# Attention, soft MoE and a gated layer on one core: one conversion step on GpSimd for two units, expert weights in 12 KB pieces, and a new place for the last rows' transposes

## The chip, the cores and the metric

One core of a Trainium2 chip runs the whole program. The metric is the device time of one execution in microseconds; the kernel before takes 594.82 us (median of 3 runs, 594.3 to 595.8). The core has five engines with instruction queues of their own, each run in order: PE (TensorE, matrix products and transposes, results in PSUM), DVE (VectorE), ACT (ScalarE), POOL (GpSimd, which here works on SBUF alone) and SP (SyncE, which here issues all the transfers).

## The reference

Three layers, one behind the other:

```python
# 1. causal attention: q, k, v are (4, 12, 448, 64)
attn = softmax(mask(q @ k.T / 8)) @ v            # -> x, (1792, 768)
# 2. soft MoE: phi (768, 32), w1 (8, 768, 1024), w2 (8, 1024, 768)
logits = x @ phi
slots  = softmax(logits, axis=0).T @ x           # 32 slots, 4 for each expert
so     = relu(slots[e] @ w1[e]) @ w2[e]          # for each of 8 experts
x      = softmax(logits, axis=1) @ so
# 3. gated layer: w_gate, w_val (768, 1536), w_out (1536, 768), given as float64
out    = (sigmoid(x @ w_gate) * (x @ w_val)) @ w_out
```

The factors that setup_inputs draws with make the weights of the third layer doubles; the kernel gets them as pairs of 32-bit words.

## The kernel before

**Attention (0 to 256 us).** Two heads make a pair, and 24 pairs run one behind the other, six for each batch. Every step of a pair (transposes of q and k `Tq`, `Tk`; their scaling to 16 bits `hq`, `hk` on ACT and the residuals `lq`, `lk` on DVE; scores; mask and row minimum `m` on DVE; exponential `e` on ACT; transposes of the probabilities `P0` to `P3` on PE with copies `C0` to `C3` out of PSUM; product with v `V`, `VZ`; two more transposes `Xa`, `Xb`) has a time in the table `AT` (L82 to L85), counted from the start of its pair. Pairs are 9.0 units apart (`II`, L81). All steps of all pairs are sorted by these times (L627) and issued in that order with every instruction pinned, so the table is the program order of each engine; only the order counts, not the values. The scores of a pair come in two lots: `S1Z` (256 keys, and the last 64 rows against 448) and `S20` (384 and 128 keys). `P3` is the transposes of the last rows. The copies C0 to C3 go to ACT or DVE by `PTE` (L79): C3 is ACT's in even pairs and DVE's in odd ones. P0 to P3, the logits `L` and the first transposes of a tail share two PSUM buffers in turn. `L` (L462) adds up the router's logits for three pairs, `LT` (L469) copies (ACT, first half of a batch) or adds them (DVE, second half). After six pairs a batch's `tail` (L506) makes the slot softmax and the sums over tokens in thirteen steps whose times stand in `TAIL` (L89).

**Expert weights (258 to 346 us).** `load_w` (L173) loads w1 and w2 in 32 transfers of 1.5 MB, each half an expert's matrix, into a ring of buffers; ten are issued during attention, the others as buffers come free. In a transfer a partition gets 3 rows of w1 (4 KB each, 128 rows apart) or 4 rows of w2 (3 KB each). For each expert, four products at a time stand side by side in PE's columns (L757 to L777). Unit 0's weights of the third layer are loaded ahead of expert 6.

**Third layer (347 to 595 us).** The 1536 hidden columns are cut into six units of 256. A unit's three matrices (`o`, `v`, `g`, 1.5 MB of doubles each, as 128 x 1536 doubles) are converted by `from_f64` (L186) in four steps: ACT builds the low word from 16 bits, ACT multiplies the high word (L196), then two bit operations on DVE (L198, L200), all in place, on every second 32-bit word. Then stage t multiplies: `gate` (L834) makes the hidden values with their 16-bit halves `hhi`, `hlo` (POOL subtracts, L852), and `outp` (L854) multiplies for each of 14 token tiles and adds into `oacc`. By `EV` (L93) the eviction is ACT's in stage 0; later it is DVE's, or ACT's with an addition on POOL (L880). While stage t runs, unit t+1 is converted. Here the order on each engine is not pinned: a planner with its own costs fixes it when the program is built.

Of the kernel before, what the change touches and what calls it, by code (L numbers as in the profile page):

```python
# [7 lines left out]
F32 = mybir.dt.float32  # L8
# [6 lines left out]
ALU = mybir.AluOpType  # L15
# [5 lines left out]
def kernel(  # L21
# [13 lines left out]
    nc = tc.nc  # L35
# [6 lines left out]
    KC = DM // 128  # L42
# [18 lines left out]
    for g, (b, h0, n) in enumerate(GRP):  # L61
        for o in range(0, n, 2):
# [18 lines left out]
    II = 9.0  # L81
    AT = dict(Tq=0.0, Tk=0.02, hk=2.66, hq=3.87, lq=4.08, lk=4.52, S1Z=6.23, m10=6.29, m11=6.34, e10=7.23, e11=7.59, mZ=7.62,  # L82
              S20=9.01, m21=10.53, m01=11.87, m00=12.14, m20=12.45, e21=13.29, e01=13.43, e00=13.47, e20=13.54, P1=13.62,
              P0=14.04, eZ=14.34, C1=15.02, C0=15.43, r=15.45, P2=15.48, P3=16.0, ri=16.52, C3=17.53, C2=18.31, V=20.55,
              VZ=20.86, xu=23.04, Xa=23.34, xn=24.26, Xb=26.29, xT=26.32, L=27.71, LT=29.3)  # L85
    LOADS = dict(q=-25.5, k=-25.4, w=-6.0, v=-1.0)
    SCALES = (-16.0, -15.0, -14.0, -11.0, -10.0, -9.0, -4.0, -2.9)
    copy = {"A": nc.scalar.copy, "V": nc.vector.tensor_copy, "P": nc.gpsimd.tensor_copy}
    TAIL = (30.3, 31.6, 32.3, 33.4, 34.6, 35.7, 41.2, 42.4, 43.6, 44.7, 46.5, 49.0, 51.0)  # L89
    PINW = True  # L90
    PB = (3, 3, 2)
    HIE = 'VAVAAAVAAAVV'
    EV = 'AAPVVPVVVPVV'  # L93
    MWE = 'AAAAAA'
    WHE = 'VVAAAV'


    const = ctx.enter_context(tc.tile_pool(name="const", bufs=1))
# [4 lines left out]
    ident = const.tile([128, 128], F32, name="ident")  # L103
# [10 lines left out]
    g = nc.gpsimd  # L114
# [27 lines left out]
    def mult(on, out, in_, x):  # L142
        if on == "A":
            nc.scalar.activation(out=out, in_=in_, func=AF.Copy, scale=x)  # L144
        else:
            nc.vector.tensor_scalar(out, in_, x, None, ALU.mult)
# [9 lines left out]
    worder = []  # L156
    for e in range(E):
        if e == E0:
            for u in PARTS[0]:
                worder += w_unit(u)  # L160
        for r in range(2):
            worder.append((("1", e, r), w1[e].rearrange("(k p) f -> p k f", p=128)[:, 3 * r:3 * r + 3, :], 3))
        for r in range(2):
            worder.append((("2", e, r), w2[e].rearrange("(k p) f -> p k f", p=128)[:, 4 * r:4 * r + 4, :], 4))
    n_ab = len(worder)
    for u in range(len(PARTS[0]), FF // UC):
        worder += w_unit(u)
# [1 line left out]
    wt = {}  # L169
# [16 lines left out]
    def from_f64(key):  # L186

        t = wt[key].bitcast(I32).rearrange("p a (b w) -> p a b w", w=2)  # L190
        lo, hi = t[:, :, :, 0], t[:, :, :, 1]
        top = wt[key].bitcast(U16).rearrange("p a (b w) -> p a b w", w=4)[:, :, :, 1]

        nc.scalar.activation(out=lo, in_=top, func=AF.Copy, scale=2.0 ** -13, bias=2.0 ** -15 - 0.5)  # L194
        yield
        mult("A", hi.bitcast(F32), hi.bitcast(F32), 2.0 ** -112)  # L196
        yield
        nc.vector.scalar_tensor_tensor(lo, hi, -2 ** 31, lo, ALU.bitwise_and, ALU.bitwise_or)  # L198
        yield
        nc.vector.scalar_tensor_tensor(hi, hi, 3, lo, ALU.logical_shift_left, ALU.bitwise_or)  # L200
        yield
        return hi.bitcast(F32)


    with ExitStack() as actx:
# [17 lines left out]
        acc = ac_p.tile([128, DM], F32, name="acc")  # L223
# [28 lines left out]
        fin = {}  # L252
# [8 lines left out]
        xu = x_p.tile([128, 512], F32, name="xu")  # L261
# [330 lines left out]
        for i in range(NP):  # L592
# [13 lines left out]
            for c in range(4):  # L606
                at(t0 + AT[f"P{c}"], st_P, i, c)
                at(t0 + AT[f"C{c}"], st_C, i, c)
            for x, f in (("r", st_r), ("ri", st_ri), ("V", st_V), ("VZ", st_VZ), ("xu", st_xu), ("Xa", st_Xa), ("xn", st_xn),
                         ("Xb", st_Xb), ("xT", st_xT)):  # L610
# [4 lines left out]
            if i % NPB == NPB - 1:  # L615
                gen([t0 + x for x in TAIL], tail, i // NPB)
        for g in range(NG):
# [12 lines left out]
        slotT = const.tile([128, KC, NS], F32, name="slotT")  # L630
        p4 = psT.tile([128, KC, NS], F32, tag="t", name="psm4")
        for kc in range(KC):
            nc.tensor.matmul(p4[:, kc], lhsT=acc[:, 128 * kc:128 * kc + 128], rhs=fin["fw"], start=True, stop=True)
        nc.vector.tensor_copy(slotT, p4)


# [120 lines left out]
    for e in range(E):  # L757
        ps = ps1.tile([128, 256], F32, tag="a", name="psh")
        for kc in range(KC):
            w = wt["1", e, kc // 3]  # L760
            for g in range(4):
                nc.tensor.matmul(ps[32 * g:32 * g + 32, :], lhsT=slotT[:, kc, :],  # L762
                                 rhs=w[:, kc % 3, 256 * g:256 * g + 256], start=kc == 0, stop=kc == KC - 1)
        hm = hm_p.tile([128, 256], F32, tag="hm", name="hm")
        nc.vector.tensor_scalar(hm, ps, 0.0, emask[:, e:e + 1], ALU.max, ALU.mult)
        pt = ps1.tile([128, 2, 128], F32, tag="b", name="psht")
        for i in range(2):
            nc.tensor.transpose(pt[:, i], hm[:, 128 * i:128 * i + 128], ident)  # L768
        hT = hm_p.tile([128, 2, 128], F32, tag="hT", name="hT")
        nc.scalar.copy(hT, pt)  # L770
        for f in range(8):
            g, i = divmod(f, 2)
            w = wt["2", e, f // 4]
            for c in range(3):
                nc.tensor.matmul(so[32 * c:32 * c + 32, :], lhsT=hT[:, i, 32 * g:32 * g + 32],  # L775
                                 rhs=w[:, f % 4, 256 * c:256 * c + 256],
                                 start=e == 0 and f == 0, stop=e == E - 1 and f == 7)  # L777
        if e < B:
            b = e
            cs = cs_p.tile([128, 4, 2, 2, NS], F32, tag="cs", name="cs")  # L780
            chi = hm_p.tile([128, 4, NS], F32R, tag="chi", name="chi")
            c = call[:, b]
            nc.vector.tensor_copy(chi, c)
            ch = chi.bitcast(F32).rearrange("p j (o s) -> p j o s", o=1).to_broadcast([128, 4, 2, NS])
            c4 = c.rearrange("p j (o s) -> p j o s", o=1).to_broadcast([128, 4, 2, NS])
            nc.vector.tensor_copy(cs[:, :, :, 0, :], ch)
            nc.vector.tensor_tensor(cs[:, :, :, 1, :], c4, ch, ALU.subtract)
            ps = ps1.tile([128, S], F32, tag="b", name="psc")
            for j, (s0, n) in enumerate(CH):
                nc.tensor.transpose(ps[:, s0:s0 + n], cs[:n, j].rearrange("p a b s -> p (a b s)"), ident[:n, :n])  # L790
            nc.scalar.copy(cT[:, b * S:(b + 1) * S], ps)
        if e == E0 - 1:
            once.close()
            wo0 = ctx.enter_context(rp("wo0", 1))
            wo_p.update({u: wo0 for u in PARTS[0]})
            w0 = {}
            for u in PARTS[0]:
                for nm in "ovg":
                    f = from_f64((nm, u))
                    while True:  # L800
                        try:
                            next(f)
                        except StopIteration as x:
                            w0[nm, u] = x.value
                            break
                for _ in prep_o(u, w0["o", u]):
                    pass
    sos = hm_p.tile([96, 256], F32, tag="sos", name="sos")
    nc.vector.tensor_copy(sos, so)
    pt = ps1.tile([128, 2, 96], F32, tag="b", name="psst")  # L810
# [148 lines left out]
```

## Time and profile before

| | |
|---|---|
| median of 3 runs | 594.82 us |
| the profiled execution | 596.93 us, its span 595.0 us |
| PE busy | 514.5 us (86%) |
| DVE busy | 390.0 us (66%) |
| ACT busy | 322.6 us (54%) |
| POOL busy | 238.7 us (40%) |
| chain that ended last | PE 63%, ACT 15%, DMA 7%, DVE 5%, issue 3%, POOL 2% |
| moved by DMA | 101.59 MB in 95566 packets, 171 GB/s over the span |

Shares are averages over three stages of different kinds, so a row is read with its stage. The chain of waits is followed back from the last instruction to whatever released each step. Line L244 stands for every pinned instruction of attention, so these are told apart by the names of their tiles: `psS` are scores, `psP` transposes of probabilities, `PT` their copies, `nm` row minima, `psL` and `LT` logits.

### The profile page before, as it was taken

The numbers are of one execution on the slowest core, as the hardware profiler recorded it, in microseconds if no ns is written. First come the engines' busy times: TensorE is split into PE (matmuls) and PEld (weight loads), VectorE is DVE, ScalarE is ACT, GpSimd is POOL, SyncE is SP. The second block draws the span as 40 slices with busy tenths as digits, with TensorE's granted clock in tenths as the row PEclk, the third lists the DMA queues.
The fourth block names the chain that finished last, engine by engine and source line by source line (L and its number), as shares of the span: only waits on it lengthen the run. The fifth ranks groups of instructions, "written<-read, shape, count | busy, mean of one in ns | idle before, by whom it ended". The sixth has DMA issues, their size and how long they took to land.

```text
span 595.0 us, 12947 instructions
## 1 busy us (share of the span) xinstructions
PE 514.5 (86%) x4971; PEld 317.2 (53%) x4971; DVE 390.0 (66%) x943; ACT 322.6 (54%) x738; POOL 238.7 (40%) x333
## 2 busy tenths in 40 slices
PE   2899989998999899799935689679999989899997
PEld 1576756665667566465512235344554445455654
DVE  3688877886878687331027038986895958675664
ACT  2577767776777577301043049996865843334300
POOL 6654663656365410000000014206696760355720
PEclk9899999999999899979995789998999979799999
DMA  7746557464774313779999993713505303000044
GB/s 161 200 106 170 167 160 199 129 144 133 199 196 115 91 33 107 287 251 391 405 397 405 405 400 137 281 38 119 200 1 209 110 2 107 0 1 1 2 185 186
DMA packets 95566, 101.59 MB, mean 171 GB/s; under 512 B 68625, under 2 KB 68625, under 8 KB 95505
## 3 DMA queue, kind: packets, MB, share of 16 engines
q1 hardware_dynamic: 95504, 100.77, 51.3%
q8 instruction: 39, 0.64, 0.5%
q14 instruction: 23, 0.18, 0.1%
HBM read 95.26 MB, written 5.51 MB: 169 GB/s over the span
## 4 chain that ended last, share of the span: by engine, by line
PE 63%; ACT 15%; DMA 7%; DVE 5%; issue 3%; POOL 2%; SPq 1%; ACTq 0%; DVEq 0%; POOLq 0%
PE pso L870 22%; PE psP L244 9%; PE psS L244 8%; DMA w<-in_moe_w_dram 6%; ACT P L244 4%; PE psX L244 4%; PE psT L244 4%; PE psh L762 3%; PE so L775 3%; ACT hi L244 3%; ACT oacc L144 2%; ACT w L194 2%; PE psg L688 2%; PE psg L843 1%; ACT w L144 1%
## 5 line engine op out<-in xcount | busy, mean ns | idle before, releaser
L852 POOL TENSOR_TENSOR hlo<-hs,hhi 128x448 f16<-128x448 f32 x48 | 59.2, 1241 | 174.9 <-DVE hhi L851 132.5
L870 PE MATMUL pso<-wh,hhi 128*128 128x384 f16 (+1 forms) x384 | 111.5, 338 | 8.1 <-ACT oacc L144 7.6
L870 PE MATMUL pso<-wl,hhi 128*128 128x384 f16 (+1 forms) x384 | 110.3, 334 | 0.0
L870 PE MATMUL pso<-wh,hlo 128*128 128x384 f16 (+1 forms) x384 | 107.8, 331 | 2.6 <-POOL hlo L852 2.6
L244 ACT ACTIVATE P<-psS,nm 128x256 f32<-128x256 f32 (+3 forms) x168 | 82.0, 504 | 31.4 <-PE psP L244 16.6
L870 PEld LDWEIGHTS <-hhi 128*128 128x128 f16 (+1 forms) x768 | 63.5, 103 | 63.8 <-issue 32.3
L244 DVE CUSTOM_DVE_ANT_0 psS<-psS,cmaskq,sc 128x256 f32<-128x256 f32 (+1 forms) x144 | 66.5, 489 | 32.7 <-PE psS L244 30.2
L882 DVE SCALAR_TENSOR_TENSOR oacc<-pso,osc,oacc 128x384 f32<-128x384 f32 x98 | 58.7, 613 | 35.1 <-PE pso L870 34.6
L244 PE MATMUL psP<-ident,P 128*128 128x128 f32 x384 | 59.6, 288 | 17.7 <-ACT P L244 11.6
L880 POOL TENSOR_TENSOR oacc<-oacc,ev 128x384 f32<-128x384 f32 x42 | 55.0, 1321 | 23.1 <-ACT ev L144 23.0
L244 PEld LDWEIGHTS psP<-ident,P 128*128 128x128 f32 x384 | 41.3, 142 | 35.9 <-ACT P L244 21.5
L244 POOL TENSOR_TENSOR sq<-sq 128x512 bf16<-128x512 bf16 (+1 forms) x88 | 56.3, 640 | 6.5
L244 PE MATMUL psV<-PT,v 128*64 128x64 f32 (+3 forms) x672 | 48.0, 293 | 0.3 <-ACT PT L244 0.3
L870 PEld LDWEIGHTS <-hlo 128*128 128x128 f16 (+1 forms) x384 | 34.1, 102 | 26.1 <-issue 3.5
L198 DVE SCALAR_TENSOR_TENSOR w<-w 128x1536 int32<-128x1536 int32 x18 | 33.7, 1874 | 14.5 <-ACT w L144 14.1
L244 PEld LDWEIGHTS psV<-PT,v 128*64 128x64 f32 x672 | 32.0, 137 | 20.9 <-issue 14.0
L144 ACT ACTIVATE ev<-pso,osc 128x384 f32<-128x384 f32 x42 | 23.6, 581 | 27.4 <-PE pso L870 23.7
L194 ACT ACTIVATE w<-w 128x1536 int32<-128x1536 uint16 x18 | 30.2, 1680 | 14.9 <-DMA w<-in_moe_w_out_dram 7.9
L244 POOL TENSOR_SCALAR r<-sum 128x7 f32<-128x7 f32 x24 | 5.9, 244 | 79.1 <-ACT P L244 71.9
L762 PE MATMUL psh<-w,slotT 128*32 128x256 f32 x384 | 29.9, 441 | 7.8 <-DMA w<-in_moe_w_dram 7.3
L244 ACT ACTIVATE hi<-psT,qks 128x448 f16<-128x448 f32 x48 | 27.8, 630 | 15.2 <-PE psT L244 15.2
L770 ACT COPY hT<-psht 128x256 f32<-128x256 f32 x8 | 3.0, 372 | 61.0 <-PE psht L768 61.0
(233 smaller groups left out, 1000.7 us busy)
## 6 DMA issues: line engine op xcount, KB each, us to landing
w<-in_moe_w_dram SPq DMA_DIRECT2D x32, 1536.0 KB, 9.3
w<-in_moe_w_out_dram SPq DMA_DIRECT2D x6, 1536.0 KB, 12.2
w<-in_moe_w_val_dram SPq DMA_DIRECT2D x6, 1536.0 KB, 13.4
w<-in_moe_w_gate_dram SPq DMA_DIRECT2D x6, 1536.0 KB, 6.7
out_dram<-oacc SPq DMA_DIRECT2D x14, 384.0 KB, 2.3
q<-in_q_dram SPq DMA_DIRECT2D x36, 128.0 KB, 3.0
k<-in_k_dram SPq DMA_DIRECT2D x36, 128.0 KB, 2.9
v<-in_v_dram SPq DMA_DIRECT2D x36, 128.0 KB, 8.0
```

Of the source, the lines that this page charges most:

```text
L144: nc.scalar.activation(out=out, in_=in_, func=AF.Copy, scale=x)
L194: nc.scalar.activation(out=lo, in_=top, func=AF.Copy, scale=2.0 ** -13, bias=2.0 ** -15 - 0.5)
L198: nc.vector.scalar_tensor_tensor(lo, hi, -2 ** 31, lo, ALU.bitwise_and, ALU.bitwise_or)
L244: x = f(*a, **kw)
L688: nc.tensor.matmul(ps[32 * g:32 * g + 32, :], lhsT=soT[:, kc], rhs=w[:, kc], start=kc < 4, stop=kc + 4 >= KC)
L762: nc.tensor.matmul(ps[32 * g:32 * g + 32, :], lhsT=slotT[:, kc, :], rhs=w[:, kc % 3, 256 * g:256 * g + 256], start=kc == 0, stop=kc == KC - 1)
L775: nc.tensor.matmul(so[32 * c:32 * c + 32, :], lhsT=hT[:, i, 32 * g:32 * g + 32], rhs=w[:, f % 4, 256 * c:256 * c + 256], start=e == 0 and ...
L843: nc.tensor.matmul(pg, lhsT=d["g"][:, cols], rhs=cT[:, b * S:(b + 1) * S], start=True, stop=True)
L852: nc.gpsimd.tensor_tensor(lo[:, c], hs, hi[:, c], ALU.subtract)
L870: nc.tensor.matmul(ps[n][o:o + m], lhsT=hid[b, u][x][:, c, s0:s0 + m], rhs=y[:, c, 384 * n:384 * n + 384], start=f, stop=l)
L880: nc.gpsimd.tensor_tensor(a, a, x, ALU.add)
L882: nc.vector.scalar_tensor_tensor(a, ps[n], osc, a, ALU.mult, ALU.add)
```

## The change

It has three parts, and changes nothing in what is computed.

1. `AT`: P3 moves from 16.0 to 18.015, behind S20 of the next pair (18.01) and ahead of Tk of the pair after it (18.02); C3 moves from 17.53 to 18.6, behind C2; LT moves from 29.3 to 30.6, from ahead of hk and the masks of 128 to between hk and hq and behind the four mask steps. The first five `TAIL` times move back by 0.2 to 1.0: the transpose `psl` from ahead of Xa to behind S1Z, the exponential `eT` from ahead of C0 to behind it.
2. Expert weights: a partition gets 3 (w1) or 4 (w2) neighbouring rows, 12 KB in one piece. Which row lies in which partition changes, so the slots' columns (stride 3), the columns of w1 that form a group (pairs, stride 4) and the columns that are transposed (stride 2) change with it.
3. `from_f64`: for units 1 and 2 the second step is POOL's, not ACT's (six instructions on 128 x 1536 words).

```diff
--- before.py
+++ after.py
@@ -81,18 +81,19 @@
     II = 9.0
     AT = dict(Tq=0.0, Tk=0.02, hk=2.66, hq=3.87, lq=4.08, lk=4.52, S1Z=6.23, m10=6.29, m11=6.34, e10=7.23, e11=7.59, mZ=7.62,
               S20=9.01, m21=10.53, m01=11.87, m00=12.14, m20=12.45, e21=13.29, e01=13.43, e00=13.47, e20=13.54, P1=13.62,
-              P0=14.04, eZ=14.34, C1=15.02, C0=15.43, r=15.45, P2=15.48, P3=16.0, ri=16.52, C3=17.53, C2=18.31, V=20.55,
-              VZ=20.86, xu=23.04, Xa=23.34, xn=24.26, Xb=26.29, xT=26.32, L=27.71, LT=29.3)
+              P0=14.04, eZ=14.34, C1=15.02, C0=15.43, r=15.45, P2=15.48, P3=18.015, ri=16.52, C3=18.6, C2=18.31, V=20.55,
+              VZ=20.86, xu=23.04, Xa=23.34, xn=24.26, Xb=26.29, xT=26.32, L=27.71, LT=30.6)
     LOADS = dict(q=-25.5, k=-25.4, w=-6.0, v=-1.0)
     SCALES = (-16.0, -15.0, -14.0, -11.0, -10.0, -9.0, -4.0, -2.9)
     copy = {"A": nc.scalar.copy, "V": nc.vector.tensor_copy, "P": nc.gpsimd.tensor_copy}
-    TAIL = (30.3, 31.6, 32.3, 33.4, 34.6, 35.7, 41.2, 42.4, 43.6, 44.7, 46.5, 49.0, 51.0)
+    TAIL = (31.3, 31.95, 33.3, 33.9, 34.8, 35.7, 41.2, 42.4, 43.6, 44.7, 46.5, 49.0, 51.0)
     PINW = True
     PB = (3, 3, 2)
     HIE = 'VAVAAAVAAAVV'
     EV = 'AAPVVPVVVPVV'
     MWE = 'AAAAAA'
     WHE = 'VVAAAV'
+    ONP = (1, 2)
 
 
     const = ctx.enter_context(tc.tile_pool(name="const", bufs=1))
@@ -159,9 +160,9 @@
             for u in PARTS[0]:
                 worder += w_unit(u)
         for r in range(2):
-            worder.append((("1", e, r), w1[e].rearrange("(k p) f -> p k f", p=128)[:, 3 * r:3 * r + 3, :], 3))
+            worder.append((("1", e, r), w1[e].rearrange("(r p k) f -> r p k f", r=2, k=3)[r], 3))
         for r in range(2):
-            worder.append((("2", e, r), w2[e].rearrange("(k p) f -> p k f", p=128)[:, 4 * r:4 * r + 4, :], 4))
+            worder.append((("2", e, r), w2[e].rearrange("(r p k) f -> r p k f", r=2, k=4)[r], 4))
     n_ab = len(worder)
     for u in range(len(PARTS[0]), FF // UC):
         worder += w_unit(u)
@@ -193,7 +194,10 @@
 
         nc.scalar.activation(out=lo, in_=top, func=AF.Copy, scale=2.0 ** -13, bias=2.0 ** -15 - 0.5)
         yield
-        mult("A", hi.bitcast(F32), hi.bitcast(F32), 2.0 ** -112)
+        if key[1] in ONP:
+            nc.gpsimd.tensor_scalar(hi.bitcast(F32), hi.bitcast(F32), 2.0 ** -112, None, ALU.mult)
+        else:
+            mult("A", hi.bitcast(F32), hi.bitcast(F32), 2.0 ** -112)
         yield
         nc.vector.scalar_tensor_tensor(lo, hi, -2 ** 31, lo, ALU.bitwise_and, ALU.bitwise_or)
         yield
@@ -630,7 +634,9 @@
         slotT = const.tile([128, KC, NS], F32, name="slotT")
         p4 = psT.tile([128, KC, NS], F32, tag="t", name="psm4")
         for kc in range(KC):
-            nc.tensor.matmul(p4[:, kc], lhsT=acc[:, 128 * kc:128 * kc + 128], rhs=fin["fw"], start=True, stop=True)
+            r, k_ = divmod(kc, 3)
+            cols = acc[:, 384 * r:384 * r + 384].rearrange("p (a k) -> p k a", k=3)[:, k_]
+            nc.tensor.matmul(p4[:, kc], lhsT=cols, rhs=fin["fw"], start=True, stop=True)
         nc.vector.tensor_copy(slotT, p4)
 
 
@@ -760,20 +766,21 @@
             w = wt["1", e, kc // 3]
             for g in range(4):
                 nc.tensor.matmul(ps[32 * g:32 * g + 32, :], lhsT=slotT[:, kc, :],
-                                 rhs=w[:, kc % 3, 256 * g:256 * g + 256], start=kc == 0, stop=kc == KC - 1)
+                                 rhs=w[:, kc % 3, 512 * (g // 2):512 * (g // 2) + 512].rearrange(
+                                     "p (a m i) -> p m a i", m=2, i=2)[:, g % 2], start=kc == 0, stop=kc == KC - 1)
         hm = hm_p.tile([128, 256], F32, tag="hm", name="hm")
         nc.vector.tensor_scalar(hm, ps, 0.0, emask[:, e:e + 1], ALU.max, ALU.mult)
         pt = ps1.tile([128, 2, 128], F32, tag="b", name="psht")
         for i in range(2):
-            nc.tensor.transpose(pt[:, i], hm[:, 128 * i:128 * i + 128], ident)
+            nc.tensor.transpose(pt[:, i], hm.rearrange("p (a i) -> p i a", i=2)[:, i], ident)
         hT = hm_p.tile([128, 2, 128], F32, tag="hT", name="hT")
         nc.scalar.copy(hT, pt)
         for f in range(8):
             g, i = divmod(f, 2)
-            w = wt["2", e, f // 4]
+            w = wt["2", e, g // 2]
             for c in range(3):
                 nc.tensor.matmul(so[32 * c:32 * c + 32, :], lhsT=hT[:, i, 32 * g:32 * g + 32],
-                                 rhs=w[:, f % 4, 256 * c:256 * c + 256],
+                                 rhs=w[:, 2 * (g % 2) + i, 256 * c:256 * c + 256],
                                  start=e == 0 and f == 0, stop=e == E - 1 and f == 7)
         if e < B:
             b = e
```

## Rows read from the trace of the kernel before

**Rows 1.** Timeline of a pair: start us, us, engine, instruction, count [idle before, releaser].

```profile
183.52 0.69 DVE L244 COPY PT<-psP 128x512 f32<-128x512 f32 x1
...
184.25 0.36 PE L244 MATMUL psS<-hi,hi 64*64 64x384 f16 x4
...
185.03 0.65 PE L244 MATMUL psT<-ident,k 128*128 128x128 f32 x4
185.26 0.62 DVE L244 CUSTOM_DVE_ANT_0 psS<-psS,cmaskq,sc 128x384 f32<-128x384 f32 x1 [1.05 <-PE psS L244]
...
185.72 1.16 ACT L244 ACTIVATE hi<-psT,qks 128x448 f16<-128x448 f32 x2 [0.78 <-PE psT L244]
...
186.70 0.63 DVE L244 CUSTOM_DVE_ANT_0 psS<-psS,cmaskq,sc 128x384 f32<-128x384 f32 x1
...
187.67 0.38 ACT L244 ACTIVATE P<-psS,nm 128x128 f32<-128x128 f32 x1
...
192.68 0.36 PE L244 MATMUL psS<-hi,hi 64*64 64x384 f16 x4
```

**Rows 2.** Chain of waits, expert stage: start us, us, what.

```profile
304.23 16.61 DMA w<-in_moe_w_dram
...
323.51 20.76 DMA w<-in_moe_w_dram
```

**Rows 3.** Busy us by stretch (PE, PEld, DVE, ACT, POOL), GLU stages t=0, t=1.

```profile
361.50:402.50 41.00, 29.91 (x205) 17.02 (x204) 35.40 (x40) 41.00 (x55) 7.22 (x5) 1.00 0.34 123
402.50:452.00 49.50, 48.08 (x310) 26.54 (x312) 40.73 (x65) 36.13 (x57) 38.67 (x30) 0.97 0.32 111
```

**Rows 4.** Timeline of ACT where it copies the logits.

```profile
168.52 0.53 ACT L244 COPY LT<-psL 96x448 f32<-96x448 f32 x1 [1.71 <-PE psL L244]
```

**Rows 5.** Timeline of ACT and PE in a batch's tail.

```profile
138.81 0.58 ACT L244 ACTIVATE P<-psS,nm 128x384 f32<-128x384 f32 x1 [0.78 <-DVE nm L244]
...
144.83 0.37 ACT L244 ACTIVATE eT<-psl,ng 128x128 f32<-128x128 f32 x1 [3.39 <-DVE ng L244]
...
146.00 0.66 PE L244 MATMUL psP<-ident,P 128*128 128x128 f32 x4 [1.71 <-ACT PT L244]
...
146.50 0.27 PE L244 MATMUL pse<-ident,eT 128*128 128x128 f32 x1
```

**Rows 6.** Stretches of full transfers; the last columns are DMA share and GB/s.

```profile
305.00:312.00 7.00, 0.00 (x0) 0.00 (x0) 3.52 (x2) 5.82 (x4) 0.00 (x0) 0.82 1.05 390
313.00:344.00 31.00, 20.25 (x173) 8.24 (x173) 10.47 (x13) 4.68 (x6) 0.00 (x0) 0.62 1.03 405
345.00:357.00 12.00, 9.59 (x62) 4.87 (x57) 5.92 (x18) 6.40 (x11) 1.72 (x2) 0.87 1.04 395
```

**Rows 7.** Lines L762 and L688: duration ns min/median/max, first and last start.

```profile
L762 PE MATMUL psh<-w,slotT x384: 379/379/637, 259.0 to 338.3; 128*32 128x256 f32 x192
...
L688 PE MATMUL psg<-w,soT x144: 385/387/418, 347.6 to 530.2; 128*32 128x256 f32 x144
```

**Rows 8.** Timeline of ACT at the last moved multiplication.

```profile
384.42 1.73 ACT L144 ACTIVATE w<-w 128x1536 f32<-128x1536 f32 x1
385.93 0.68 ACT L144 ACTIVATE oacc<-pso,osc 128x384 f32<-128x384 f32 x1
```

**Rows 9.** GpSimd's instructions by shape: busy us, mean ns, idle before.

```profile
L244 POOL TENSOR_TENSOR sq<-q 128x512 bf16<-128x512 f32 x22 | 22.5, 1042 | 4.5 <-ACT sq L244 3.8
...
L226 POOL MEMSET cmask<- 128x448 f32 x1 | 0.5, 475 | 0.0
```

**Rows 10.** Timeline of GpSimd beside the conversions.

```profile
370.92 1.05 POOL L852 TENSOR_TENSOR hlo<-hs,hhi 128x448 f16<-128x448 f32 x1 [0.33 <-DVE am L137]
378.00 3.65 POOL L852 TENSOR_TENSOR hlo<-hs,hhi 128x448 f16<-128x448 f32 x1 [6.04 <-ACT hhi L851]
...
431.33 8.77 POOL L880 TENSOR_TENSOR oacc<-oacc,ev 128x384 f32<-128x384 f32 x5 [0.60 <-ACT ev L144]
```

**Rows 11.** Line L198, the conversion's DVE step: ns min/median/max.

```profile
L198 DVE SCALAR_TENSOR_TENSOR w<-w x18: 1744/1759/2575, 308.1 to 502.4; 128x1536 int32<-128x1536 int32 x18
```

## The prediction, made before the changed kernel was run

> **What bounds the kernel now.** I read the busy shares by stretch first, then the chain of waits, then the timelines of the places that the diff touches. There are three regimes. Attention (to about 256 us) is a ring of PE and ACT: in a plain pair the scores of 384 follow each other at 184.25 and 192.68, 8.43 us [rows 1]. The ring runs through the transposes of k (185.03), the two scalings of q and k on ACT, which start as soon as those end (185.72, after 0.78 us of idling for PE), ACT's exponentials, and back to PE. DVE is not in it: it idles 1.05 us before its first mask step at 185.26. Expert weights (300 to 345 us) are bound by transfers: the chain holds two waits for expert weights, 16.61 and 20.76 us [rows 2]. GLU from 352 us: while unit 0 is multiplied out (t=0, to 402.5 us), ACT is busy 41.00 of 41.00 us, DVE 35.40 and PE only 29.91; in the next stage PE is busy 48.08 of 49.50 [rows 3]. So t=0 is ACT's. What a change gains in any of the three moves the end, since the next regime is late by as much; later stages are PE's and can't give it back except through what is pushed into them.
>
> **Part 1, attention order.** P3 (four transposes, about 0.5 us of PE) moves from before Xb to between the scores of 384 and the transposes of k; its copy C3 moves from behind the last mask step to behind C2. PE's work between two transposes of k stays the same, so the ring itself gains nothing: k's transposes end when they did, and ACT starts its scalings then. What changes is DVE. In odd pairs C3 is DVE's (0.69 us at 183.52, in time that DVE has free [rows 1]) and is queued ahead of the mask steps. It now waits for P3, which ends when k's transposes start, 185.03. It then runs at about 185.2 and the first mask step at 185.85 in place of 185.26: 0.6 us later. The fourth mask step goes from 186.70 to 187.3, its sum is read at 188.0, and the exponential that reads the same bank goes from 187.67 to 188.05 [rows 1]: +0.38 us on the ring. Of 12 odd copies, 4 fall in pairs where ACT is late anyway (next paragraph): 8 x 0.38 = +3.0 us. In even pairs C3 is ACT's and ends as k's transposes do: 0.
>
> LT is ACT's four times and DVE's four times (once in the last, serial tail). On ACT it idles 1.71 us for the logits and then takes 0.53 us ahead of both scalings [rows 4]. At 30.6 it stands between them, so one scaling (half of 1.16 us [rows 1]) goes first: 4 x 0.58 = -2.3 us. On DVE it now stands behind all four mask steps, so the 0.78 us that the first exponential waits for them at 138.81 goes [rows 5]; the logits' reductions, which free a PSUM buffer that P0 needs, still stand behind both residual steps, so I count only the 0.55 us by which the scores come earlier.
>
> In the tails the batch's exponential eT stands on ACT ahead of C0 and idles 3.39 us; P3 therefore waits 1.71 us for C0 [rows 5]. At 33.9 it stands behind C0. That stall goes. Next late is the transpose of eT, which can't run before 144.83 + 0.37 + 0.2 = 145.4, against 146.50 now: 1.1 us, of which P3, now behind it, takes 0.5 back. With the 0.55 us from LT that is 1.15 us in each of three tails: -3.5 us. The last tail has nothing beside it and is a chain of its own: 0. The other moved steps (the transpose psl behind the scores of the next pair, POOL's memset) pass work with slack; the w loads and POOL's sums on SP and POOL keep their place. Attention: +3.0 - 2.3 - 3.5 = **-2.8 us**; -5.8 if the odd copies cost nothing, +2.5 if all 12 cost and the tails gain nothing.
>
> **Part 2, 12 KB pieces.** 32 expert transfers fall from 384 or 512 pieces (4 or 3 KB) to 128. No piece of 12 KB is in the trace. With 3 and 4 KB pieces 405 GB/s were moved (313 to 344 us), with 2 KB pieces 390, with 6 and 2 KB 395 [rows 6]; the DMA share is over 1.0 in all three. A fixed cost per piece fitted to 390 at 2 KB and 405 at 3.5 KB (7 ns a piece) gives 420 GB/s at 12 KB. Attention issues ten of the 32 transfers; the other 22 are 34.6 MB, 85 us at 405, so this end is -3.0 us. The other end is the slowest rate seen, 390: +3.3 us. The 6 KB pieces show no gain over 3 or 4, so I take -0.5.
>
> The Trainium skill's page "DMA: Bandwidth & Descriptors", section "Why small descriptors are slow (HBM only)", puts about 3 cycles on each packet beside one per 32 bytes: 131/128 at 4 KB, 387/384 at 12 KB, an estimate of 1.5 to 2.3%, or -1.3 to -2.0 us in place of -0.5. Its section "Where 436 GB/s comes from" says that HBM binds at about 358 GB/s, by which pieces would change nothing; the trace disagrees with that figure, at 405.
>
> The matmuls that read these weights now step: 8 bytes out of 16. The nearest row is the same product on converted weights, read 4 bytes out of 8: 387 ns against 379 [rows 7]. An expert has 48 such half-products, four at a time: 12 x 8 ns = 0.1 us, under the wait for transfers: 0. The stepped reads of acc (6 products) and hm (16) at 2%: under 0.1. If stepped reads took twice as long, the first buffer would come free half an expert's product later, at most 6 x 0.38 = 2.3 us, and the queue of transfers with it: +2 us at most.
>
> **Part 3, six multiplications to GpSimd.** Unit 1's and unit 2's lie at 357 to 386 us, one of the six before 361.5. The last takes 1.73 us on ACT, 1.51 to the next start [rows 8]: 5 x 1.5 = 7.5 us less, so ACT would need 33.5 us for the stretch of 41. GpSimd has no such operation in the trace. Below it is a fill of 448 elements in 475 ns, 1.06 ns each; above, a product of two inputs over 512 in 1042, 2.03 ns each [rows 9]. For 1536: 1.6 to 3.1 us. One input and one output lie between, 2.4 us.
>
> It isn't free, though: a subtraction that takes 1.05 us at 370.92 took 3.65 at 378.00 while DVE worked on two SBUF inputs, and five additions took 8.77 us at 431.33 [rows 10]; the conversion's DVE step, 1.76 us, has gone up to 2.58 [rows 11]. I treat the two as taking turns. In 361.5 to 402.5 DVE has 15 such steps x 1.76 = 26.4, one more of 1.8, and GpSimd 5 subtractions x 1.05 = 5.2: 33.4 us. With 5 x 2.4 = 12.0 it is 45.4, over the 41 there are. But four of the DVE steps (7.0 us) are unit 3's, not due before two stages later; DVE has 49.5 - 40.7 = 8.8 us free in the next stage [rows 3]. If these slip, the sum is 38.4, less what overlaps (the 8.77 us at 431 held five additions of about 1.0 and 2.6 of DVE's steps, 9.5 us of both: 8%): 35.4. So t=0 shortens by 2.6 to 5.6 us, at most 7.5 (ACT again). I take **-4.0**. Behind the longer conversion stand GpSimd's later subtractions, which the products four tiles on wait for; that lead, 4 x 50.5/14 = 14 us, covers 2 to 5 us.
>
> Sum: -2.8 - 0.5 - 4.0 = -7.3 us on a profiled execution of 596.93 us (span 595.0), which lies 2.1 us above the median of 594.82. I set the same difference on the median: **587.5 us**.
>
> **Rivals.**
> A. Turns at SBUF eat t=0: unit 3's steps stay in place, the sum is 45.4 less 8%, about 41.7, so t=0 keeps its 41. Left is -2.8 - 0.5: 591.5. For: DVE has an order fixed before the run. Against: ACT is what stands in front of unit 1.
> B. All of it: -5.8, -1.5 (half the fitted gain), -7.5: 580. For: ACT is full without a gap. Against: the odd copies have 0.6 us less on DVE by the rows.
> C. Slower: the multiplication runs at the rate of two inputs, 3.1 us, and only in DVE's gaps, and unit 3's steps stay: 33.4 + 15.6 = 49 us in place of 41, +8; with attention at -2.8 about 600. It decides from (41 - 33.4)/5 = 1.5 us a piece with unit 3's steps, 2.9 without. The Trainium skill speaks for it: "GPSIMD Engine Reference", sections "Specifications" and "When to use GPSIMD", has GpSimd share its SBUF interfaces with VectorE, in contention with DVE instructions of two SBUF inputs, and advises VectorE for elementwise work; the 3.65 us at 378.00 agree.
> D. A wash: the odd copies cost in all pairs, and A holds: about 595.
>
> **How the numbers follow.** Forecast 0.45, A 0.17, B 0.12, D 0.09, C 0.17. Range 580 to 600 (the forecast alone 584 to 591). About 0.3%, 1.8 us, is what a measurement can tell from no change. Faster: nearly all of the forecast and B, three quarters of A, 0.70; slower: C and a little of D, 0.19; the same 0.11.
>
> **What would show it.** Plain pairs at 8.4 us for even copies and 8.8 for odd; P3's stall of 1.71 us gone from three tails; transfers at 405 to 410 GB/s; six GpSimd steps of 2 to 5 us; ACT below full in t=0 and t=0 under 50.5 - 2.6 us. Plain pairs shorter than 8.4 us, or DVE full in t=0 with PE still idle for 11 of 41 us, would make the prediction wrong.

## The result and the profile after

The changed kernel takes 598.25 us (median, 596.0 to 601.9) against 594.08 for the kernel before, run beside it: 1.0079 of it, 95% interval 1.0059 to 1.010. The forecast was 587.5 and faster; it came out slower by 0.8%, inside the range and on the side of rival C. The profiled execution took 598.1 us (span 596.3).

The page of the changed kernel: busy time by engine, then the span in 40 slices of 14.9 us, in tenths.

```profile
PE 515.5 (86%) x4971; PEld 317.9 (53%) x4971; DVE 408.5 (69%) x943; ACT 313.5 (53%) x732; POOL 268.5 (45%) x339
...
DVE  3687787887877877421053059999597798875664
ACT  2577766776777767101170078088576774334300
POOL 6655753756466410000000059753678682355720
```

DVE has gained 18.5 us of busy time although nothing was given to it. Its instructions got longer, in the slices where GpSimd now works (DVE's four nines, slices 25 to 28, 358 to 417 us).

**Where the time went**, read at three marks. The last scores of 384 start at 230.93 us (before 234.46): attention gained 3.5. ACT loads its table for the first gate at 345.31 (351.70): expert weights gained another 2.9. The table below gives the first start of `hs`, the first DVE step of a gate, in each stage.

| first `hs` of unit | 0 | 1 | 2 | 3 | 4 | 5 |
|---|---|---|---|---|---|---|
| before | 353.6 | 403.4 | 439.0 | 480.1 | 515.9 | 547.3 |
| after | 347.2 | 401.5 | 449.6 | 487.2 | 517.2 | 548.6 |
| no_pool (below) | 348.0 | 396.8 | 434.9 | 473.5 | 506.9 | 538.4 |

From 6.4 us ahead the changed kernel falls to 10.6 us behind at unit 2; the two stages after that are 3.5 and 5.8 us shorter than before and give 9.3 of these 17 back.

A first `hs` is not the same point of the work in every kernel. Unit 0's last eviction starts 1.3 us ahead of unit 1's first `hs` before, 0.5 us behind it in no_pool, but 8.2 us behind it in the changed kernel. Evictions of unit 0 (duration ns min/median/max, first and last start), before, changed kernel, no_pool:

```profile
L144 ACT ACTIVATE oacc<-pso,osc x28: 573/690/750, 360.6 to 402.1; 128x384 f32<-128x384 f32 x28
```

```profile
L145 ACT ACTIVATE oacc<-pso,osc x28: 555/580/649, 354.5 to 409.7; 128x384 f32<-128x384 f32 x28
```

```profile
L145 ACT ACTIVATE oacc<-pso,osc x28: 572/680/742, 355.0 to 397.3; 128x384 f32<-128x384 f32 x28
```

Counted from unit 0's first `hs`, the last of these starts after 48.5, 62.5 and 49.3 us. So unit 0 itself is late by 13 to 14 us, and what the table shows as lost between units 1 and 2 is in part the rest of unit 0.

**Attention.** An odd pair's timeline in the changed kernel, where [rows 1] showed one before (start us, us, engine, instruction, count [idle before, releaser]).

```profile
183.26 0.38 PE L248 MATMUL psS<-hi,hi 64*64 64x384 f16 x4
...
184.56 0.60 PE L248 MATMUL psT<-ident,k 128*128 128x128 f32 x4
184.76 0.69 DVE L248 COPY PT<-psP 128x512 f32<-128x512 f32 x1 [1.64 <-PE psP L248]
185.20 1.16 ACT L248 ACTIVATE hi<-psT,qks 128x448 f16<-128x448 f32 x2 [1.05 <-PE psT L248]
185.37 0.62 DVE L248 CUSTOM_DVE_ANT_0 psS<-psS,cmaskq,sc 128x384 f32<-128x384 f32 x1
...
186.80 0.63 DVE L248 CUSTOM_DVE_ANT_0 psS<-psS,cmaskq,sc 128x384 f32<-128x384 f32 x1
...
187.58 0.37 ACT L248 ACTIVATE P<-psS,nm 128x128 f32<-128x128 f32 x1
...
192.14 0.52 PE L248 MATMUL psS<-hi,hi 64*64 64x384 f16 x4
```

The reader is to see the copy of P3 on DVE waiting 1.64 us for PE and the mask right behind it: this pair takes 8.88 us, 8.43 before. Now the tail that [rows 5] showed.

```profile
145.05 0.37 ACT L248 ACTIVATE eT<-psl,ng 128x128 f32<-128x128 f32 x1 [1.95 <-DVE ng L248]
...
145.56 0.33 PE L248 MATMUL pse<-ident,eT 128*128 128x128 f32 x1 [0.95 <-ACT eT L248]
```

`pse` starts 0.94 us earlier, and no P3 ahead of it waits for a copy any more.

**Stage t=0.** Busy us by stretch (PE, PEld, DVE, ACT, POOL, each with its instructions; granted clock, DMA share, GB/s), placed as far behind the first gate as in [rows 3].

```profile
355.00:396.00 41.00, 25.39 (x158) 12.74 (x157) 39.32 (x28) 22.38 (x35) 37.08 (x12) 0.83 0.33 121
396.00:445.50 49.50, 44.09 (x266) 22.69 (x265) 42.12 (x57) 37.38 (x55) 23.96 (x18) 0.97 0.27 100
```

ACT went from 41.00 to 22.38; five multiplications are 7.5 us of that, the rest is work that came later. DVE is at 39.32 with 28 instructions (35.40 with 40 before), GpSimd at 37.08 and PE idles 15.6 of 41 us. The timeline of GpSimd, DVE and PE in that stage shows who holds whom:

```profile
350.89 4.45 POOL L198 TENSOR_SCALAR w<-w 128x1536 f32<-128x1536 f32 x1
351.10 0.67 DVE L857 SCALAR_TENSOR_TENSOR hs<-psv,v0s,sg 128x448 f32<-128x448 f32 x1
...
355.37 2.57 DVE L202 SCALAR_TENSOR_TENSOR w<-w 128x1536 int32<-128x1536 int32 x1 [3.60 <-POOL w L198]
...
358.81 10.20 POOL L198 TENSOR_SCALAR w<-w 128x1536 f32<-128x1536 f32 x2
360.98 3.90 DVE L858 CAST hhi<-hs 128x448 f16<-128x448 f32 x1
...
369.73 2.48 DVE L204 SCALAR_TENSOR_TENSOR w<-w 128x1536 int32<-128x1536 int32 x1
...
370.56 5.72 POOL L198 TENSOR_SCALAR w<-w 128x1536 f32<-128x1536 f32 x1
372.69 4.40 DVE L147 TENSOR_SCALAR wh<-w,w1s 128x1536 f16<-128x1536 f32 x1
...
377.94 5.72 POOL L198 TENSOR_SCALAR w<-w 128x1536 f32<-128x1536 f32 x1
379.51 4.85 DVE L202 SCALAR_TENSOR_TENSOR w<-w 128x1536 int32<-128x1536 int32 x1
384.29 0.67 DVE L857 SCALAR_TENSOR_TENSOR hs<-psv,v0s,sg 128x448 f32<-128x448 f32 x1
385.01 3.63 PE L694 MATMUL psg<-w,soT 128*32 128x256 f32 x24 [12.24 <-DVE hs L857]
```

The two engines take turns, and both wait. A conversion step, a cast of 448 words or `wh` that starts inside a multiplication ends just behind it: `wh` at 372.69 + 4.40 = 377.09, the multiplication at 370.56 + 5.72 = 376.28. The cast at 360.98, 0.38 us elsewhere, takes 3.90. `hs`, which reads one of its inputs from PSUM, isn't held (0.67 us at 351.10). The other way round, a multiplication that starts while such a DVE step is under way is late too: two of the six take 4.44 and 4.45 us, four take 5.72 to 5.84, as the one at 370.56, beside the step that ends at 369.73 + 2.48 = 372.21.

The chain of harm ends on PE: `hs` at 384.29 stands behind these steps in DVE's queue, it holds the PSUM buffer that unit 1's product needs, and PE waits 12.24 us for it, with the rest of unit 0 queued behind. After that wait, in which PE did nothing, the granted clock of 385 to 389 us is 0.50, the lower of its two levels, and the 24 products take 3.63 us; in no_pool 12 of them take 1.10 us at 1.00.

The DVE groups of 345 to 410 us (count | busy us, mean ns | idle before), first of the changed kernel, then of no_pool, the same kernel with the six multiplications back on ACT:

```profile
L202 DVE SCALAR_TENSOR_TENSOR w<-w 128x1536 int32<-128x1536 int32 x8 | 21.0, 2625 | 3.7 <-POOL w L198 3.6
L204 DVE SCALAR_TENSOR_TENSOR w<-w 128x1536 int32<-128x1536 int32 x7 | 15.9, 2277 | 0.0
L858 DVE CAST hhi<-hs 128x448 f16<-128x448 f32 x5 | 5.5, 1107 | 0.0
L147 DVE TENSOR_SCALAR wh<-w,w1s 128x1536 f16<-128x1536 f32 x1 | 4.4, 4402 | 0.0
```

```profile
L202 DVE SCALAR_TENSOR_TENSOR w<-w 128x1536 int32<-128x1536 int32 x8 | 14.9, 1861 | 4.0 <-ACT w L145 4.0
L204 DVE SCALAR_TENSOR_TENSOR w<-w 128x1536 int32<-128x1536 int32 x8 | 14.3, 1784 | 0.1
L858 DVE CAST hhi<-hs 128x448 f16<-128x448 f32 x7 | 3.8, 536 | 0.0
...
L147 DVE TENSOR_SCALAR wh<-w,w1s 128x1536 f16<-128x1536 f32 x1 | 1.0, 1011 | 0.0
```

Per instruction, 8 x 0.76 + 7 x 0.49 + 5 x 0.57 + 3.4 = 15.8 us of the same DVE work are waiting; unit 0's last eviction is 13.2 us later behind the unit's first `hs` than in no_pool. That a conversion's third step gets its input later is hardly the cause: for that DVE idles 3.6 us here, and 4.0 us for ACT in no_pool.

### The profile page after: what moved, and what is told of

The parts are those of the page before. It is cut to its first block, busy times and chain, and to the rows that moved or that the text cites. A ratio compares the mean times of both kernels' runs of the same rounds, so it can differ in the third digit from the quotient of the medians.

```text
span 596.3 us, 12962 instructions
## 1 busy us (share of the span) xinstructions
PE 515.5 (86%) x4971; PEld 317.9 (53%) x4971; DVE 408.5 (69%) x943; ACT 313.5 (53%) x732; POOL 268.5 (45%) x339
## 4 chain that ended last, share of the span: by engine, by line
PE 56%; DVE 18%; ACT 9%; DMA 8%; issue 5%; POOL 1%; ACTq 0%; DVEq 0%; POOLq 0%
PE pso L877 16%; PE psP L248 9%; PE psS L248 8%; DVE w L202 4%; PE so L782 4%; PE psX L248 4%; PE psh L768 4%; ACT P L248 3%; DMA w<-in_moe_w_val_dram 3%; DVE w L204 3%; DMA w<-in_moe_w_dram 3%; PE psT L248 3%; DVE psS L248 2%; DMA w<-in_moe_w_gate_dram 2%; DVE hs L857 2%
## 5 line engine op out<-in xcount | busy, mean ns | idle before, releaser
L859 POOL TENSOR_TENSOR hlo<-hs,hhi 128x448 f16<-128x448 f32 x48 | 61.3, 1283 | 145.3 <-DVE hhi L858 129.1
L877 PE MATMUL pso<-wh,hhi 128*128 128x384 f16 (+1 forms) x384 | 109.8, 334 | 6.9 <-ACT oacc L145 3.2
L877 PE MATMUL pso<-wl,hhi 128*128 128x384 f16 (+1 forms) x384 | 108.3, 329 | 0.0
L248 PE MATMUL psP<-ident,P 128*128 128x128 f32 x384 | 64.5, 291 | 11.8 <-ACT P L248 10.2
L887 POOL TENSOR_TENSOR oacc<-oacc,ev 128x384 f32<-128x384 f32 x42 | 51.5, 1240 | 27.3 <-ACT ev L145 27.2
L202 DVE SCALAR_TENSOR_TENSOR w<-w 128x1536 int32<-128x1536 int32 x18 | 41.1, 2283 | 16.5 <-ACT w L145 12.8
L248 ACT COPY PT<-psP 128x512 f32<-128x512 f32 x60 | 35.6, 594 | 12.6 <-PE psP L248 12.6
L248 DVE COPY PT<-psP 128x512 f32<-128x512 f32 x36 | 24.6, 684 | 20.0 <-PE psP L248 18.5
L204 DVE SCALAR_TENSOR_TENSOR w<-w 128x1536 int32<-128x1536 int32 x18 | 36.6, 2032 | 0.1
```

What stands on the lines that cost most here:

```text
L248: x = f(*a, **kw)
L859: nc.gpsimd.tensor_tensor(lo[:, c], hs, hi[:, c], ALU.subtract)
L877: nc.tensor.matmul(ps[n][o:o + m], lhsT=hid[b, u][x][:, c, s0:s0 + m], rhs=y[:, c, 384 * n:384 * n + 384], start=f, stop=l)
L887: nc.gpsimd.tensor_tensor(a, a, x, ALU.add)
```

## The experiments

**The parts one by one.** no_pool is the changed kernel without part 3; pool_only, order_only and pieces_only are the kernel before with one part each.

```diff
-    ONP = (1, 2)
+    ONP = ()
```

> The changed kernel with the second conversion step back on ACT for units 1 and 2; parts 1 and 2 stay. Theory T (the six GpSimd multiplications alone cost the time: each holds GpSimd 4.4 to 5.8 us and keeps DVE's conversion steps and casts waiting): attention's -3.5 us (last scores of 384 at 230.9 in place of 234.5) and the expert stage's -2.7 us (gating starts 6.4 us earlier than before) reach the end, so about 594.1 - 6.2 = 588 us, ratio 0.990. Rival R (the later stages give back whatever comes early, since PE or the planner's order binds there): 594 us or more, ratio 1.00. Rival S (the loss sits in the new order or pieces, not on GpSimd): 597 to 599 us.

> The kernel before with only the six multiplications moved to GpSimd. Theory T: t=0 (first eviction wait to last eviction of unit 0) grows from 51 to about 64 us, of which later stages give back some 6: +7 us, about 601 us, ratio 1.012; the GpSimd steps take 4.4 to 5.8 us each. Rival S (the loss comes from the new order or pieces): 594 us, ratio 1.00.

> The kernel before with only part 1, the new order of attention. Theory T: last scores of 384 near 230.9 us in place of 234.5, plain pairs with an even copy 8.35 us and with an odd copy 8.87 us, and the 3.5 us reach the end: 590.6 us, ratio 0.994. Rival R (transfers bound the expert stage, which started its queue during attention, and take the gain back): 594 us, ratio 1.00.

> The kernel before with only part 2, the 12 KB pieces. Theory T: 412 to 420 GB/s in the full stretch in place of 405, gating of the third layer starts about 2.7 us earlier, 591.4 us, ratio 0.9955. Rival (the stepped reads of w1 hold PE, or the rate was given by attention's earlier end): 594 us, ratio 1.00, with 405 GB/s.

| | us | of the kernel before, 95% interval |
|---|---|---|
| no_pool | 586.24 | 0.9861 (0.9833 to 0.9888) |
| pool_only | 605.34 | 1.0189 (1.0158 to 1.0220) |
| order_only | 589.47 | 0.9921 (0.9894 to 0.9949) |
| pieces_only | 593.17 | 0.9973 (0.9953 to 0.9993) |

Singly the parts are worth -0.79, -0.27 and +1.89%; the sum, +0.83%, is what the whole change measured (+0.79%). So part 3 alone turned the sign: parts 1 and 2 together, in no_pool, give -1.4%. Theory T named the right side in all four, but not each size: pool_only cost 4 us more than the 601 us expected, no_pool and order_only gained 1 to 2 us more (last scores of 384 at 229.4 and 229.5 us in place of 230.9), and pieces_only 1.8 us less. Busy time and rate of transfers by stretch, pieces_only and then order_only, which keeps the 3 and 4 KB pieces:

```profile
275.00:285.00 10.00, 10.00 (x146) 5.64 (x142) 1.11 (x3) 0.90 (x2) 0.00 (x0) 1.00 1.01 427
...
325.00:335.00 10.00, 5.21 (x76) 2.31 (x72) 0.00 (x0) 0.00 (x0) 0.00 (x0) 1.00 1.02 429
```

```profile
275.00:285.00 10.00, 10.00 (x154) 5.91 (x154) 1.11 (x3) 1.79 (x4) 0.00 (x0) 1.00 1.03 404
...
325.00:335.00 10.00, 5.17 (x78) 2.25 (x72) 0.48 (x1) 0.00 (x0) 0.00 (x0) 1.00 1.03 405
```

The six stretches from 275 to 335 us have a mean of 420 GB/s with 12 KB pieces and 402 without.

**The price by itself.** A program of its own with pinned steps: GpSimd's and DVE's instructions in turn, then beside each other.

```diff
+    nc.gpsimd.tensor_scalar(hi[:, :m], hi[:, :m], 2.0, None, ALU.mult)
+    nc.vector.tensor_copy(hh, h)
```

> A program of its own: it leaves the whole computation out and only runs the disputed instructions one group behind the other on 128 x 1536 words, first alone and then with GpSimd and DVE side by side. Theory T (the moved multiplication is slow by itself, and excludes DVE while it runs): alone 4.4 us, as at 350.89 us of the changed kernel, and beside it DVE's 448-word cast, 0.38 us alone, ends only when the multiplication does (about 4 us), and three conversion steps (1.75 us each alone) take some 4 us more together. Theory L (it is fast alone, 2.4 us as the prediction had it, and only DVE's work on SBUF stretches it): 2.4 us alone, 4.4 to 5.8 beside DVE. By T the step's stride (one word in two) may matter: read without gaps it would be half as long; if the cost is the operation's, the same.

Timeline of the probe: a multiplication, an addition of two inputs and a copy on GpSimd, a bit step and a cast on DVE, each alone; then a multiplication beside three DVE bit steps, and one beside three casts.

```profile
15.06 4.20 POOL L64 TENSOR_SCALAR A<-A 128x1536 f32<-128x1536 f32 x1 [14.64 <-DVE J L60]
...
36.82 3.42 POOL L73 TENSOR_TENSOR C<-C,X 128x1536 f32<-128x1536 f32 x1
...
40.50 1.46 POOL L76 COPY C<-X 128x1536 f32<-128x1536 f32 x1 [0.26 <-DVE J L60]
...
42.27 1.75 DVE L79 SCALAR_TENSOR_TENSOR W<-W 128x1536 int32<-128x1536 int32 x1
...
44.20 0.39 DVE L82 CAST hh<-h 128x448 f16<-128x448 f32 x1
...
45.88 4.22 POOL L64 TENSOR_SCALAR A<-A 128x1536 f32<-128x1536 f32 x1 [3.91 <-DVE J L60]
45.90 8.48 DVE L79 SCALAR_TENSOR_TENSOR W<-W 128x1536 int32<-128x1536 int32 x3
...
54.53 4.20 POOL L64 TENSOR_SCALAR A<-A 128x1536 f32<-128x1536 f32 x1 [4.44 <-DVE J L60]
54.56 5.27 DVE L82 CAST hh<-h 128x448 f16<-128x448 f32 x3
```

The multiplication takes 4.20 us, whether it steps over every second word or not (4.08 contiguous), as theory T had it. In the probe GpSimd always starts first, by 0.02 to 0.03 us, and DVE pays: three casts go from about 1.1 to 5.27 us, 4.2 more, all of the multiplication, and three bit steps from 3 x 1.75 = 5.25 to 8.48, 3.2 more, so about 1 us of the first ran beside it. The probe's last group was to put an ACT step in GpSimd's place, but that step had run at 8.89 us, long before, so the probe says nothing on ACT; in the kernel before the bit step's median is 1.76 us [rows 11], with ACT busy for 41.00 of 41.00 us [rows 3]. The Trainium skill's page "SBUF — State Buffer", section "SBUF: two separate sides", says that the port pair of VectorE and GpSimd is "an exclusive lock, not a bandwidth split": against a DVE instruction with two SBUF inputs or in a two-port mode, whichever starts first has it for the whole instruction. The casts here agree, and so do the multiplications of 5.72 to 5.84 us above; of the bit steps' time all but that 1 us does.

**One unit at a time**, to see whether the loss goes with the number of steps.

```diff
-    ONP = (1, 2)
+    ONP = (1,)     # unit1; (2,) in unit2
```

> The changed kernel with GpSimd taking the second step for unit 1 only; unit 2's is ACT's again. Against 586.2 us without any and 598.3 with both. Theory O (the loss comes through PE's fixed order: unit 1's products of weights stand ahead of unit 0's tiles in PE's queue, and PE waits 12 us for the late conversion of unit 1): nearly all the loss, 595 to 598 us. Theory T (each piece costs its own time on GpSimd and DVE): half of it, 592 us.

> The changed kernel with GpSimd taking the second step for unit 2 only. Theory O: unit 2 isn't needed until the next stage, so nothing in front of PE is late and ACT is relieved of three steps: 583 to 587 us. Theory T: half of the loss, 592 us.

unit1 took 595.9 us, 1.0037 (1.0007 to 1.0067), unit2 595.03, 1.0022 (0.9994 to 1.0050). Each costs 1.6 to 1.8% over no_pool, both together 2.2%: not in proportion. The expectation from the order alone gave 583 to 587 for unit2 and fell; half of the loss, 592 us, fell in both. unit2 loses its 7 us by the first `hs` of unit 1 (403.8, 396.8 in no_pool); unit1 loses 4.3 there (401.1) and five more by that of unit 2 (444.4, 434.9 in no_pool). In both, unit 0's last eviction starts at 398.5 or 398.8 us, 397.3 in no_pool, so here it is unit 1 that comes late, not unit 0. In unit2 something in front of PE was late after all: DVE's last conversion step for unit 1, at 371.85 us, ran into GpSimd's step for unit 2 (371.08, 4.99 us) and took 4.91 us.

**Order or price.** Since the planner fixes each engine's order from its own costs, a moved step also changes the order: unit 1's first product stands behind 5 of unit 0's 14 tiles in no_pool and behind 8.67 in the changed kernel. pool_copy keeps the changed kernel's order nearly whole (8.67 again) and takes most of the price away, by a copy that turns 16-bit into 32-bit words in place of the multiplication, which it leaves out; dve_step gives the multiplications to DVE.

```diff
-            nc.gpsimd.tensor_scalar(hi.bitcast(F32), hi.bitcast(F32), 2.0 ** -112, None, ALU.mult)
+            nc.gpsimd.tensor_copy(hi.bitcast(F32), wt[key].bitcast(U16).rearrange("p a (b w) -> p a b w", w=4)[:, :, :, 3])
+            mult("V", hi.bitcast(F32), hi.bitcast(F32), 2.0 ** -112)     # dve_step, in place of the line above
```

> The changed kernel with GpSimd's six multiplications replaced by six copies of 128x1536 (16-bit words read, 32-bit words written, in the same places): the multiplication itself is left out, so the third layer computes on other weights. The planner gives it nearly the order of the changed kernel (unit 1's first product behind 8.67 tiles of unit 0 in both; 5.0 without the GpSimd steps), so order and price come apart. Theory P, the price of the GpSimd step and what it holds up on DVE sets the loss (a copy took 1.46 us by itself where the multiplication took 4.20): t=0 ends at about 398 as without the steps, and the kernel takes 585 to 590 us, 0.985 to 0.993 of the kernel before. Theory O, the order that the planner made for the GpSimd steps sets it: PE still waits about 12 us for unit 1's weights, and the kernel takes 595 to 599 us, 1.002 to 1.008.

> The changed kernel with the six multiplications of units 1 and 2 on DVE (about 1.0 us each by the row of the weights' first 16-bit half) in place of GpSimd. Theory P (ACT bounds t=0, and 1.5 us a piece off ACT is worth something if what takes it over is short and takes no turns with DVE): DVE goes from 35.4 to about 40 of 41 us, so t=0 gains 0 to 3 us against the kernel without the GpSimd steps: 583 to 587 us, 0.981 to 0.988 of the kernel before. Theory O (any other order than the one with the steps on ACT loses): 590 us or more, above 0.992.

pool_copy took 589.65 us, 0.9896 (0.9858 to 0.9935): of the 2.2% between no_pool and the changed kernel 1.8 go with the price, and 0.35, within the intervals, stay. The copies take 1.76 us (median), and unit 1 begins at 392.4 us. PE's wait for `hs`, and the DVE groups of 345 to 410 us, which are nearly back:

```profile
376.23 3.59 PE L694 MATMUL psg<-w,soT 128*32 128x256 f32 x24 [3.97 <-DVE hs L857]
```

```profile
L204 DVE SCALAR_TENSOR_TENSOR w<-w 128x1536 int32<-128x1536 int32 x8 | 15.8, 1969 | 0.0
L202 DVE SCALAR_TENSOR_TENSOR w<-w 128x1536 int32<-128x1536 int32 x8 | 14.8, 1856 | 1.5 <-POOL w L198 0.9 <-ACT w L145 0.6
L858 DVE CAST hhi<-hs 128x448 f16<-128x448 f32 x7 | 4.4, 634 | 0.0
```

In t=0 itself the order keeps a larger part: unit 0's last eviction starts at 400.7 us, 54.5 behind the unit's first `hs`, where the changed kernel has 62.5 and no_pool 49.3. So 8 of the 13.2 us there go with the price and 5 stay; at the end of the span 1.9 of these are left.

dve_step took 584.33, 0.9835 (0.9806 to 0.9863), as expected; its first `hs` of units 0 and 1 are at 346.8 and 393.0 us, 46.3 apart, against 48.8 in no_pool. On DVE one takes this (line, shapes, count | busy us, mean ns):

```profile
L147 DVE TENSOR_SCALAR w<-w 128x1536 f32<-128x1536 f32 x6 | 6.6, 1095 | 0.0
```

The engine that is fullest after ACT does the step in a quarter of GpSimd's time and costs less.

**The odd copies.** c3_act is no_pool with the odd pairs' C3 on ACT, c3_dve is dve_step with the same.

```diff
-    PTE = "AVAAAVAV"
+    PTE = "AVAAAVAA"
```

> The changed kernel without the GpSimd steps, and with the copy C3 of odd pairs on ACT in place of DVE. Theory of the odd copies (C3 in DVE's queue ahead of the masks costs 0.45 us a plain odd pair): plain odd pairs at 8.4 us in place of 8.87, 8 x 0.45 = 3.6 us less than 586.2: 582.6 us. Rival (ACT's order binds as well: C3 then stands ahead of the scalings and delays them): pairs of 8.8 us, 586 us or more.

> The two best edits together: the new order and the 12 KB pieces, the odd pairs' copies C3 on ACT, and the six multiplications of units 1 and 2 on DVE. If the two are independent (one shortens attention, the other t=0), the ratios multiply: 0.9821 from the copies on ACT, and 0.9835/0.9861 = 0.9974 from the multiplications on DVE in place of ACT, so 0.9795, about 581.8 us of the 594 of the kernel before; between 0.976 and 0.983. If what DVE saves in t=0 had only come from DVE being late in attention, the second factor goes: 0.982 or more.

c3_act took 582.5 us, 0.9821 (0.9780 to 0.9862), the best of all: plain odd pairs take 8.53 to 8.56 us in place of 8.88. That the time expected, 582.6, was met is in part luck: the pairs didn't reach 8.4 us, attention from the third pair on is 2.1 us shorter (193.3 for 195.4), not 3.6, and the intervals of c3_act and no_pool overlap. c3_dve, meant to add the two, took 585.77, 0.9876 (0.9848 to 0.9905); above the 0.976 to 0.983 expected. The other reading on record, 0.982 or more, covers the number but doesn't say why c3_act's own gain shrinks. Its attention is as short (first expert product at 251.6, in c3_act 251.1), but by the first `hs` stage t=1 takes 41.9 us and t=2 39.3, in dve_step 40.7 and 35.8, in c3_act 42.0 and 37.1. I did not find what makes these stages longer or shorter from build to build; the order on the engines differs in each. Five kernels here convert by the same steps (before, order_only, pieces_only, no_pool, c3_act), and in their profiled executions the time from the first `hs` to the end of the span is 235.2 to 241.4 us. So gains of 0.3% between single builds, that of dve_step over no_pool among them, aren't read as shown. The four kernels with multiplications on GpSimd lie outside that spread, at 245.9 to 249.3 us; pool_copy has 241.8.

## Why the prediction was wrong, step by step

- **What bounds each stage: right** for attention, expert weights and t=0, and each gain moved the end, as argued: -1.4% without part 3. That the later stages "can't give it back" held for the gains, not for the loss: of the 17 us lost by unit 2 they gave back 9.3.
- **Part 1, direction and pieces right, size too small: -2.8 forecast, -4.7 (3.0 to 6.3) measured in order_only.** From the third pair to the last, attention takes 199.2 to 199.3 us in the three kernels with the old order and 195.4 to 195.5 in the seven with the new one that leave C3 on DVE: -3.8. The first two pairs vary by themselves, between 17.1 and 19.2 us, so that in the two profiles shown first attention gained only 3.5. Six of the seven plain odd copies there cost 0.42 to 0.64 us a pair (0.38 argued), one nothing, and even pairs 0.1 or less. The copy of the logits gives 0.55 (0.58). The mis-sized term is the three tails: 1.0, 1.3 and 2.5 us, 4.7 in place of 3.5. c3_act takes back 0.32 us a plain odd pair, so most of the cost of the odd copies is the copy on DVE.
- **Part 2, mis-sized.** The fit of a fixed cost per piece gave 420 GB/s and -3.0 us; I set it down to -0.5 because 6 KB pieces showed no gain. 420 is what was measured, and in the profiles the first gate comes 2.3 us (pieces_only) to 2.9 earlier. The median gained 0.27% (0.07 to 0.47), 1.6 us.
- **Part 3, the step that failed: "One input and one output lie between, 2.4 us."** The multiplication costs 4.20 us alone and 4.44 to 5.84 in the kernel, more than an operation with two inputs (3.42). The upper bound, 3.1 us from two inputs, was no bound: GpSimd's time for 1536 words depends on the operation (1.46, 3.42 and 4.20 us in the probe), and the trace of before held no multiplication by a constant of that size. The rule that the two engines take turns held, in both directions. With 4.3 in place of 2.4 the prediction's own sum is 33.4 + 5 x 4.3 = 54.9 us, 14 over the 41 there are, or 44 to 48 us with unit 3's steps out.
- **"If these slip": they did, and it didn't help.** Unit 3's four DVE steps, at 392.5 to 399.4 us before, start at 403.8 to 411.7, behind unit 1's first `hs`. In the 41 us of the stretch above, 9 conversion steps start where the prediction counted 15, and DVE is full all the same. That fits the sum with these steps out, 3 to 7 us over: unit 1's first `hs` lies 54.3 us behind unit 0's, 48.8 in no_pool. The 14 us are met only by unit 0's last eviction (13.2), for another reason, the next one.
- **The cover of 14 us for the gates' later steps was not one, and this is the second step that failed.** It counted products four tiles on; what ended last was a PSUM buffer that `hs` frees, and in PE's queue unit 1's product, which waited 12.24 us for it, stood ahead of the last five of unit 0's tiles. Nor did the sum weigh that every DVE instruction behind a held one waits too.
- **Rival C** had the side, the place and nearly the time (600), the time in part by luck: its t=0 was 8 us longer where 14 were measured, with 9.3 given back later. Half of its mechanism is there: a multiplication waits for a DVE step that is under way, but not for a gap, and DVE's steps wait for the multiplications. The rate of two inputs was too fast, and unit 3's steps didn't stay.
- **The signs named.** Of the two that would make the prediction wrong, the second, DVE full with PE idle for 11 of 41 us, came: 39.32 us busy, and 15.6 idle. The first, plain pairs under 8.4 us, tells nothing: even pairs take 8.33 to 8.48 us, and some took 8.36 before. The stall of P3 and the odd pairs came as said; t=0 got longer, the GpSimd steps took 4.4 to 5.8 us (2 to 5 said) and transfers ran at 403 to 429 GB/s in pieces_only (405 to 410).
- **Two smaller sums are off:** 12 odd copies at 0.38 us with nothing from the tails give +2.3, not +2.5, and rival D comes to 593 us by its own terms, not 595.
- **Open:** why either unit's three steps alone cost nearly as much as all six, and what the order adds by itself: 5 us of t=0 and 0.35% of the whole in pool_copy. An order held fixed across builds would tell; it wasn't tried.

## What to carry to other kernels

Before a step goes to an idle engine, measure that very operation there and count its time against the neighbour that shares its port as well: here 6 x 1.5 us off ACT cost about 16 us of DVE. Ask as well what stands behind the held instruction in every queue: the loss came out on PE, in tiles that needed none of the moved work. A bound taken from another operation, even a seemingly heavier one, is no bound. Where a planner orders the queues, time a copy of the same shape in the step's place: it separates the price from the new order, as far as the planner keeps that order.

## What was not expected of the hardware

- On GpSimd 1536 words a partition take 1.46 us to copy, 3.42 to add from two inputs and 4.20 to multiply by a constant (2.19 for 768, 1.20 for 384: 2.6 ns a word). The Trainium skill's "GPSIMD Engine Reference", section "Engine selection", has operations with one input "roughly line-rate": true of the copy here, not of the multiplication.
- A DVE cast of 448 words, 0.38 us, took 3.90 because it started during such an instruction; GpSimd's own time stayed at 4.20 to 4.22 beside DVE in the probe, where it started first, and went to 5.72 to 5.84 in the kernel, where a DVE step was under way at its start.
- In stretches of 10 us, 12 KB pieces moved 403 to 429 GB/s, where 3 and 4 KB pieces moved 398 to 405.
